# A gated mix of softmax attention and a feature-map attention on one core: 91 instead of 79 offloaded exponential packs, with other rules and values for the planner

## The chip, the cores and the metric

The kernel runs on 1 core of one Trainium2 chip. The metric is the device time of one launch in microseconds, the median of several runs. The profile is one execution, taken by the hardware profiler; its span is the time from the first to the last instruction on the core.

## The reference

Cut and shortened. Two attention branches share one input of 2048 rows and 512 columns in bfloat16, with 32 heads of 16 columns. Branch A is softmax attention: 32 heads x 2048 x 2048 scores are exponentiated. Branch B is a linear attention whose feature map is a softmax over 16 columns. A gate for each row mixes the two.

```python
def _A_ref(x, wqkv, wo):
    q, k, v = ...                                   # (1, 32, 2048, 16) each
    scores = jnp.einsum("bhqd,bhkd->bhqk", q, k) * (Dh ** -0.5)
    p = _softmax(scores, axis=-1)
    o = jnp.einsum("bhqk,bhkd->bhqd", p, v)
    return o.transpose(0, 2, 1, 3).reshape(B, S, D) @ wo

def _B_ref(x, wqkv, w_phi, wo):
    pq, pk = q @ w_phi, k @ w_phi                   # per head, 16 x 16
    phi_q = concatenate([softmax(pq), softmax(-pq)])
    phi_k = concatenate([softmax(pk), softmax(-pk)])
    kv, z = phi_k^T v, sum of phi_k over s
    return (phi_q kv / (phi_q z + 1e-6)) @ wo

g = sigmoid((x * gate_w).sum(-1))
return g * _A_ref(...) + (1 - g) * _B_ref(...)
```

## The kernel before, in words

**Tiles.** Branch A goes through 32 tiles n, each of 512 queries (one of four chunks) and four heads. A tile has 16 key blocks kt of 128 keys; a key block has four score matrices of 128 keys x 512 queries, one for each head, which are called units. The main chain (main_chain, line 831 on) takes units in groups of 2 and 3. For each group TensorE writes the scores to a ring of five PSUM banks (ps_ring, L885), ScalarE exponentiates them to a ring of 20 slots in SBUF (ET, L903), and TensorE multiplies them with the values, which have a column of ones for the row sums, into ps_ot (L942). At a tile's end VectorE transposes ps_ot (L1079) and divides by the row sums (L1081, L1082, L1090).

**Packs.** Some key blocks of a tile do not go to ScalarE: dve_pack (line 970 on) takes a whole key block, four units, through VectorE and GpSimd. DVE_COUNT says how many packs a tile has, 79 in all. The steps of a pack:

- four score matmuls into the two banks of ps_mp (L992), each evacuated by VectorE to 32-bit integers EW, scaled so that the upper half holds the exponent and the lower half the fraction (L997);
- Ef, the fraction as a float16 (L1024), in pieces of 512 or 1024 columns. The planner may put each piece on GpSimd or on VectorE; SHAPE and PIECES give the sizes;
- ED, the exponent part shifted to bfloat16's place (L1028), on GpSimd alone, in pieces of 512 or 1024 columns;
- a polynomial in Ef on VectorE in three steps that depend on each other: Em = Ef x Ef (L1033), Em = E3 x Em + E1 (L1035), Ef = Ef x Em as an integer (L1037);
- a DMA with integer addition, issued by GpSimd, that adds Ef onto ED in SBUF (L1040, 512 KB); ED, read as bfloat16, is then the exponential;
- four matmuls with the values into ps_ot (L1050).

There are 2 buffers of EW, 3 of Ef, 3 of ED and one of Em; packs follow each other in order through Em (ed_prev).

**Other work.** The projections of q, k and v (L728, L807 with their evacuations L745, L777, L812, L827), the whole of branch B (feature, query_b) and the output projection (L1269, L1290) are spread over the same time. Branch B uses VectorE (L1204, L1206, L1236 to L1240), ScalarE (L1192) and transposing DMAs on the SP queue (L1212, L1245). The SP queue also places q by DMA (L763).

**The planner.** No order is written out by hand. Each step is an operation with an engine, an estimated duration, a release time, a priority, the buffers that it takes and frees, and what it depends on. Sched.run is a list scheduler: it steps through modelled time and always gives the engine that is free first its ready operation of lowest priority number. The order in which it places operations is the order of each engine's instructions; times exist only in the model, and on the chip each instruction waits for semaphores. Fillers (L961, spare_mm) are zero matmuls that the planner puts in TensorE's idle time.

The planner models one shared resource of VectorE and GpSimd, which it calls the port: operations on SBUF data (port=True on VectorE, all of GpSimd's) exclude each other, through hold["dve"] and hold["pool"]. An operation with gate=True is parked until VectorE has work that does not need the port, or has nothing to do, for long enough; it is then also made to wait for the VectorE instruction ahead of that gap (c.war.append(last)). In the kernel before, the DMA of a pack is such an operation.

What a DMA costs in the model comes from SWD = [issue on GpSimd in us, bytes, latency in us]; bytes are spread at 250 KB/us over a common DMA time, so that later DMAs queue behind earlier ones. A pack's release and priority come from its tile's start and end in modelled time (tn), LEAD[0] and LEAD[1], and from the tables by tile OFF, PRI, POLY; LEAD[6] is the priority offset of its last matmuls. AFF, SHY, FILL and SLIP are thresholds by tile in the scheduler's choices.

The time of the chain's start and the length of a unit in the model are PACE.

## Time and profile before

| | |
|---|---|
| median of 3 runs | 875.87 us (872.78 to 876.44) |
| the profiled execution's own time | 876.78 us |
| its span | 874.9 us |
| mean granted TensorE clock | 0.988 |
| instructions | 15147 |
| DMA moved | 67.46 MB, mean 77 GB/s |

The profile names engines PE (TensorE matmuls), PEld (its weight loads), DVE (VectorE), ACT (ScalarE), POOL (GpSimd) and SP (SyncE, whose queue issues DMAs). A row of a group gives line, engine, operation, output and input with shapes, the count, and then busy time in us, mean duration of one in ns, and the idle time of the engine ahead of them with what ended most of it. Busy time is a union: instructions that overlap on one engine count once, so that busy time divided by the count is what one instruction costs in a dense run, and is below its mean duration. In the waits a row is who waited, for whom, and then us in total, times, and the longest. In a time line a row is start, length, engine, line, and in brackets the engine's idle time just before and what ended it. In the busy time by stretch a row is the stretch, its length, then the busy time of PE, PEld, DVE, ACT and POOL with instruction counts, the granted clock, the DMA engines' share and GB/s.

### The profile page before, as it was taken

What the parts mean: (1) busy time and instruction counts of PE and PEld (TensorE: products, weight loads), DVE (VectorE), ACT (ScalarE), POOL (GpSimd) and SP (SyncE); (2) the same over time, 40 slices, a digit from 0 to 9 for tenths busy, and PEclk for the clock granted to TensorE, in tenths of its full rate; (3) what the DMA queues carried; (4) which work ended last, traced back from release to release, by engine and by line L of the source; (5) the groups of instructions that cost most, each with busy time, mean ns of one, the idle gap of its engine ahead of it and who ended that gap; (6) DMA issues with size and microseconds to landing.
All of it is one profiled execution on the core that took longest, in us unless ns stands there. A gap on an engine that the chain in (4) does not pass through costs nothing.

```text
span 874.9 us, 15147 instructions
## 1 busy us (share of the span) xinstructions
PE 798.2 (91%) x6241; PEld 237.8 (27%) x6241; DVE 719.8 (82%) x1030; ACT 822.0 (94%) x765; POOL 322.3 (37%) x394
## 2 busy tenths in 40 slices
PE   8989999899999999899997899988988998989998
PEld 3333322233333322222221222222222222222222
DVE  6889889867679998995984998889788898988843
ACT  6995999999999999699996999899999999999997
POOL 2425344411114433433441454322435444363421
PEclk9998999999999999999997999999999999999999
DMA  6352541534324444544155334544423525432331
GB/s 141 78 91 61 100 72 31 98 64 76 64 52 93 82 82 82 103 82 94 40 105 67 64 65 90 82 88 70 94 58 68 103 49 88 83 76 52 76 73 49
DMA packets 94292, 67.46 MB, mean 77 GB/s; under 512 B 76560, under 2 KB 84112, under 8 KB 94224
## 3 DMA queue, kind: packets, MB, share of 16 engines
q0 software_dynamic: 11376, 41.42, 24.7%
q1 hardware_dynamic: 81504, 24.55, 14.8%
q8 instruction: 49, 0.80, 0.4%
q10 hardware_dynamic: 1344, 0.52, 0.2%
q14 instruction: 19, 0.16, 0.1%
HBM read 3.69 MB, written 2.10 MB: 7 GB/s over the span
## 4 chain that ended last, share of the span: by engine, by line
ACT 74%; DVE 9%; DMA 8%; PE 8%; issue 1%; POOL 0%; SPq 0%; POOLq 0%
ACT ET L903 70%; DMA ED<-Ef 5%; ACT phi L1192 3%; DVE EW L997 3%; PE ps_ring L885 2%; DMA phiT<-phi 2%; PE ps_ot L942 1%; DVE Ef L1024 1%; PE ps_ot L961 1%; DVE Em L1033 1%; DVE T L1082 1%; PE ps_mp L992 1%; PE ps_mp L728 1%; PE ps_ot L1050 1%; DMA WA<-in_A_wqkv_dram 1%
## 5 line engine op out<-in xcount | busy, mean ns | idle before, releaser
L903 ACT ACTIVATE ET<-ps_ring 128x1024 bf16<-128x1024 f32 (+1 forms) x693 | 793.0, 1314 | 40.9 <-PE ps_ot L942 22.6
L885 PE MATMUL ps_ring<-qT,kT 64*128 64x512 bf16 x1732 | 347.1, 386 | 45.4 <-ACT ET L903 34.2
L1028 POOL TENSOR_SCALAR ED<-EW 128x512 int16<-128x512 int16 (+1 forms) x256 | 210.5, 888 | 267.0 <-DVE Ef L1037 88.9
L997 DVE TENSOR_SCALAR EW<-ps_mp 128x512 int32<-128x512 f32 x316 | 204.7, 683 | 44.9 <-PE ps_mp L992 43.9
L961 PE MATMUL ps_ot<-zero,iden 64*128 64x512 bf16 (+2 forms) x680 | 152.7, 381 | 0.0
L885 PEld LDWEIGHTS ps_ring<-qT,kT 64*128 64x128 bf16 x1732 | 72.0, 93 | 286.6 <-ACT ET L903 263.5
L1040 POOL DMA_DIRECT2D ED<-Ef x79 | 70.9, 913 | 191.3 <-DVE Ef L1037 62.0
L942 PE MATMUL ps_ot<-ET,Vaug 128*17 128x512 bf16 x1732 | 136.5, 384 | 1.5 <-DVE T L1079 1.5
L992 PE MATMUL ps_mp<-qT,kT 64*128 64x512 bf16 (+1 forms) x316 | 112.5, 387 | 8.3 <-DVE EW L997 4.0
L1033 DVE TENSOR_TENSOR Em<-Ef 128x2048 f16<-128x2048 f16 x79 | 101.7, 1288 | 2.2 <-POOL Ef L1024 1.4
L1037 DVE TENSOR_TENSOR Ef<-Ef,Em 128x2048 int16<-128x2048 f16 x79 | 97.4, 1233 | 0.8
L1024 DVE TENSOR_SCALAR Ef<-EW 128x1024 f16<-128x1024 uint16 (+1 forms) x121 | 85.1, 713 | 3.2 <-DMA ED<-Ef 2.8
L1024 POOL TENSOR_SCALAR Ef<-EW 128x1024 f16<-128x1024 uint16 (+1 forms) x51 | 48.0, 941 | 78.2 <-DVE EW L997 47.9
L1035 DVE TENSOR_SCALAR Em<-Em 128x2048 f16<-128x2048 f16 x79 | 58.6, 742 | 0.9
L961 PEld LDWEIGHTS ps_ot<-zero,iden 64*128 64x128 bf16 (+2 forms) x680 | 48.3, 96 | 37.7 <-issue 1.1
L942 PEld LDWEIGHTS ps_ot<-ET,Vaug 128*17 128x17 bf16 x1732 | 26.7, 87 | 80.1 <-issue 68.1
L992 PEld LDWEIGHTS ps_mp<-qT,kT 64*128 64x128 bf16 (+1 forms) x316 | 28.9, 95 | 63.4 <-DVE EW L997 34.5
L1206 DVE TENSOR_TENSOR phi<-phi,frec 128x1024 bf16<-128x1024 bf16 x32 | 42.1, 1317 | 0.3
L728 PE MATMUL ps_mp<-Wp,xT 128*128 128x512 bf16 x128 | 39.3, 384 | 0.3 <-DVE EW L997 0.2
L728 PE MATMUL ps_mp<-xT,WA 128*128 128x512 bf16 (+1 forms) x128 | 38.0, 378 | 1.1 <-DMA WA<-in_A_wqkv_dram 0.6
L1192 ACT ACTIVATE phi<-ps_mp 128x512 bf16<-128x512 f32 x64 | 37.2, 679 | 1.0 <-PE ps_mp L728 1.0
L1050 PE MATMUL ps_ot<-ED,Vaug 128*17 128x512 bf16 x316 | 31.5, 389 | 6.2 <-DMA ED<-Ef 6.0
(90 smaller groups left out, 398.5 us busy)
## 6 DMA issues: line engine op xcount, KB each, us to landing
ED<-Ef POOLq DMA_DIRECT2D x79, 512.0 KB, 4.8
qT<-qst SPq DMA_DIRECT2D x120, 16.0 KB, 1.8
out_dram<-outt SPq DMA_DIRECT2D x12, 128.0 KB, 1.7
WA<-in_A_wqkv_dram SPq DMA_DIRECT2D x3, 384.0 KB, 4.4
phiT<-phi SPq DMA_TRANSPOSE x48, 3.2
WBV<-in_B_wqkv_dram SPq DMA_DIRECT2D x1, 512.0 KB, 6.5
Wp<-in_A_wo_dram SPq DMA_DIRECT2D x1, 512.0 KB, 4.1
WBV<-in_B_wo_dram SPq DMA_DIRECT2D x1, 512.0 KB, 5.9
```

What stands on the lines that cost most here:

```text
L728: m = s.op("pe", self.c_mm(n), lambda e, c=c: e.matmul(self.bk(b)[:, 0:n], lhs(c), rhs(c), start=(c == 0), stop=(c == 3)), deps if c == 0 ...
L885: return lambda e: e.matmul(self.ps_ring[:, x % RING, :], self.kT[r, g // 2, kt * P:(kt + 1) * P], self.qT[r, n % 2, i, :], start=True, st ...
L903: self.o_exp.append(s.op("act", w * 0.434 + 0.045, lambda e, b0=b0, s0=s0, w=w: e.activation(self.ET[:, s0:s0 + w, :], self.ps_ring[:, b0: ...
L942: return lambda e: e.matmul(self.ps_ot[32 * i:32 * i + VSL, :], self.Vaug[:, kt, h, :], self.ET[:, (4 * p + k) % NSLOT, :], start=(kt == 0 ...
L961: return lambda e: e.matmul(self.ps_ot[c:c + nc, :], self.iden[r:r + nr, 0:nc], self.zero[r:r + nr, :], start=False, stop=False, tile_posi ...
L992: return lambda e: e.matmul(bank(), self.kT[r, cp, kt * P:(kt + 1) * P], self.qT[r, n % 2, i, :], start=True, stop=True, tile_position=(r. ...
L997: return s.op("dve", dur, lambda e: e.tensor_scalar(self.EW[:, ew.idx, x * QCH:(x + w) * QCH], src(), float(EC), float(127 * 65536), op0=A ...
L1024: fs = [s.op("pool", U * 8.26e-4 + 0.28, lambda e, c=c: e.tensor_scalar(self.Ef[:, ef.idx, U * c:U * c + U], half(0, dt.uint16, c, U), flo ...
L1028: hs = [s.op("pool", W * 8.26e-4 + 0.165, lambda e, c=c: e.tensor_scalar(self.ED[:, ed.idx, W * c:W * c + W].bitcast(dt.int16), half(1, dt ...
L1033: u = s.op("dve", 1.13, lambda e: e.tensor_tensor(self.Em[:], Ef(), Ef(), ALU.mult), fs + [self.ed_prev], pr, port=True)
L1037: g_ = s.op("dve", 1.13, lambda e: e.tensor_tensor(Ef().bitcast(dt.int16), Ef(), self.Em[:], ALU.mult), [q], pr, port=True)
L1040: v = s.op("pool", SWD[0], lambda e: e.dma_start(out().bitcast(dt.int16), Ef().bitcast(dt.int16), accum_op=ALU.add), [g_] + hs, pr, frees= ...
```

## The change

The change has four parts. DVE_COUNT gives 13 tiles one or two packs more and two tiles one less, 91 packs in all for 79. The planner no longer counts a DMA on GpSimd as a user of the port. The DMA of a pack is no longer gated. And SWD and the tables have other values: the model's issue takes 0.65 us instead of 1.1, the latency 1.6 us instead of 2.5, and the bytes are 662500 instead of 524288; packs are released 30 us ahead of their place in the tile instead of 16.5 (LEAD[0]), with 5.0 instead of 8.7 added for their priority (LEAD[1]). No instruction computes anything else than before, and no buffer is added.

```diff
-LEAD = [16.455462617506317, 8.705434360851719, 19.141216454617272, 18.856826992452106, 21.376333972175523, 40.540151693083416, 4.775252756783429, 13.0]
-PACE = [0.8933644759852923, 0.45802931388055307]
+LEAD = [30.0, 5.0, 19.141216454617272, 18.856826992452106, 21.376333972175523, 40.540151693083416, 4.775252756783429, 13.0]
+PACE = [0.8749384591637832, 0.45792738439677627]
...
-SWD = [1.1, 524288, 2.5]
+SWD = [0.65, 662500, 1.6]
...
-DVE_COUNT = (1, 3, 2, 2, 2, 3, 2, 2, 1, 2, 3, 3, 2, 3, 2, 3, 2, 3, 3, 2, 3, 3, 2, 3, 3, 2, 3, 3, 3, 3, 3, 2)
+DVE_COUNT = (1, 3, 3, 2, 3, 4, 2, 2, 1, 3, 4, 2, 3, 2, 3, 3, 4, 3, 3, 3, 3, 3, 3, 3, 3, 3, 3, 3, 3, 3, 4, 3)
...
-        self.port = port or eng == "pool"
+        self.port = port or (eng == "pool" and not dma)
...
         v = s.op("pool", SWD[0], lambda e: e.dma_start(
             out().bitcast(dt.int16), Ef().bitcast(dt.int16), accum_op=ALU.add), [g_] + hs, pr, frees=[ef],
-            gate=gate, dma=SWD[1])
+            dma=SWD[1])
```

One of RULES and many of the values of AFF (all zero before), OFF, PRI, SHY, FILL, SLIP, POLY and SHAPE differ too. What all of this makes of the program is seen in the order of its instructions, which is known before it runs. By the order, the changed kernel has 338 exponentials of two units and 336 of three (before 347 and 346), 91 of each of L1033, L1035, L1037 and L1040 (before 79), 364 evacuations L997 (316), 104 wide and 41 narrow Ef pieces on VectorE (109 and 12), 40 wide and 35 narrow ones on GpSimd (35 and 16), 300 ED pieces (256), and 463 fillers (680). SP's queue has the same DMAs.

Three places show how the order moves. The first is GpSimd's queue in the middle of the program, around the DMA of the last pack of tile 18 (tiles count from 0), the first of the pair here; ED and Ef are the pack's buffers, whose numbers are left out. Before:

```order
L1028 TENSOR_SCALAR ED<-EW 128x512
L1040 DMA ED<-Ef 128x2048
L1024 TENSOR_SCALAR Ef<-EW 128x1024 x2
L1028 TENSOR_SCALAR ED<-EW 128x1024 x2
L1040 DMA ED<-Ef 128x2048 x2
L1028 TENSOR_SCALAR ED<-EW 128x1024 x2
L1040 DMA ED<-Ef 128x2048
```

And now, around the same pack, whose DMA is the second of the two here:

```order
L1024 TENSOR_SCALAR Ef<-EW 128x1024
L1028 TENSOR_SCALAR ED<-EW 128x512 x3
L1040 DMA ED<-Ef 128x2048
L1024 TENSOR_SCALAR Ef<-EW 128x1024
L1028 TENSOR_SCALAR ED<-EW 128x512
L1040 DMA ED<-Ef 128x2048
L1028 TENSOR_SCALAR ED<-EW 128x512 x3
```

Two DMAs that stood behind each other now have conversions of a following pack between them. Before, 10 of the 79 DMAs directly follow another one; now none does.

The second place is VectorE's queue ahead of the second transposition of ps_ot (L1079), the end of tile 1; gden, gcol, wphi and Wp belong to the gate and to branch B's weights. Before:

```order
L1033 TENSOR_TENSOR Em<-Ef 128x2048
L1035 TENSOR_SCALAR Em<-Em 128x2048
L1037 TENSOR_TENSOR Ef<-Ef,Em 128x2048
L1112 TENSOR_SCALAR gden<-gneg 128x16
L1113 RECIPROCAL gcol<-gden 128x16
L812 CAST Vaug<-ps_mp 128x4x8x16
L997 TENSOR_SCALAR EW<-ps_mp 128x512 x2
L1116 TENSOR_TENSOR wphi<-wphc,m_52 128x512
L997 TENSOR_SCALAR EW<-ps_mp 128x512 x2
L1024 TENSOR_SCALAR Ef<-EW 128x512
L1130 CAST Wp<-ps_mp 128x4x128
L997 TENSOR_SCALAR EW<-ps_mp 128x512 x4
```

Two L1130 and the transposition follow. And now:

```order
L1033 TENSOR_TENSOR Em<-Ef 128x2048
L1035 TENSOR_SCALAR Em<-Em 128x2048
L1037 TENSOR_TENSOR Ef<-Ef,Em 128x2048
L1079 STREAM_TRANSPOSE T_77<-ps_ot 128x512
L1112 TENSOR_SCALAR gden<-gneg 128x16
L1081 RECIPROCAL rinv<-T_77 128x16
L1113 RECIPROCAL gcol<-gden 128x16
L1116 TENSOR_TENSOR wphi<-wphc,m_52 128x512
```

The transposition has moved ahead of the gate, of the weights and of the next packs' evacuations. Ahead of the first transposition (not shown) stand three whole chains L1033 to L1037 now, and two before.

The third place is VectorE's queue at the end of tile 17. Before:

```order
L1033 TENSOR_TENSOR Em<-Ef 128x2048
L1290 TENSOR_SCALAR outt<-ps_mp,gcol 128x512
L1035 TENSOR_SCALAR Em<-Em 128x2048
L1037 TENSOR_TENSOR Ef<-Ef,Em 128x2048
L1024 TENSOR_SCALAR Ef<-EW 128x1024
L1079 STREAM_TRANSPOSE T_77<-ps_ot 128x512
L1081 RECIPROCAL rinv<-T_77 128x16
L997 TENSOR_SCALAR EW<-ps_mp 128x512 x4
```

And now, at the same transposition:

```order
L1033 TENSOR_TENSOR Em<-Ef 128x2048
L997 TENSOR_SCALAR EW<-ps_mp 128x512 x2
L1035 TENSOR_SCALAR Em<-Em 128x2048
L1024 TENSOR_SCALAR Ef<-EW 128x1024
L997 TENSOR_SCALAR EW<-ps_mp 128x512 x3
L1079 STREAM_TRANSPOSE T_77<-ps_ot 128x512
L1081 RECIPROCAL rinv<-T_77 128x16
L1037 TENSOR_TENSOR Ef<-Ef,Em 128x2048
```

Between the steps of a chain there now stand evacuations and conversions of later packs. L1035 directly follows its L1033 in 7 of 91 chains, before in 27 of 79; behind L1037 comes an evacuation L997 in 34 cases, a conversion L1024 in 19.

More of the change, by code (lines that the diff above doesn't have):

```diff
@@ L30 @@
 PASSES = 1
-LEAD = [16.455462617506317, 8.705434360851719, 19.141216454617272, 18.856826992452106, 21.376333972175523, 40.540151693083416, 4.775252756783429, 13.0]
-PACE = [0.8933644759852923, 0.45802931388055307]
+LEAD = [30.0, 5.0, 19.141216454617272, 18.856826992452106, 21.376333972175523, 40.540151693083416, 4.775252756783429, 13.0]
+PACE = [0.8749384591637832, 0.45792738439677627]
 BOUNDS = [3.0710501327799653, 8.000889564597248, 7.971137937737645, 18.02257936663145, 29.86797202712817]
-RULES = [0.14805191866515324, 0.5274031413498357, 0.09512931304184667]
+RULES = [0.1498235423970469, 0.5274031413498357, 0.09512931304184667]
 PIECES = ((2, 2), (2, 4), (4, 4))
@@ new lines @@
+PRI = [-2.5977761809841518, 12.575398704445774, 3.895376356683779, 2.074886791441081, -6.1760123019027215, 0.0, 0.4457880973056989, 12.368950578623885, 7.524264789393655, -1.888923368598384, -5.057883055897609, 4.784017942556362, 0.7346491630142227, 0.0, 2.0007432723814103, 0.0, -8.964017875209546, -6.817875849305981, -12.903739516547825, 10.87669422388445, 2.941617488397717, -4.250877620548464, 5.900872194940888, -12.246670183932817, -8.652806589559093, 2.1291175144482652, -5.675434887761552, -0.8975021592515438, -7.6958394115627495, -4.167683124616095, -8.873737501331755, 12.096931011196038, 0.0]
@@ L49 @@
+SHAPE = [2, 0, 2, 2, 2, 1, 1, 2, 2, 1, 1, 0, 0, 1, 0, 0, 2, 1, 0, 1, 0, 0, 0, 1, 1, 0, 1, 1, 1, 0, 1, 2, 1]
 VSL = 17
```

14 lines of the change are left out of this document (6 added, 8 removed).

## The prediction

> **What bounds the kernel now.** I read the page first, then ScalarE's waits and time line, then the busy time by stretch. From the page, the busy times and the chain that ended last:
>
> ```profile
> PE 798.2 (91%) x6241; PEld 237.8 (27%) x6241; DVE 719.8 (82%) x1030; ACT 822.0 (94%) x765; POOL 322.3 (37%) x394
> ...
> ACT 74%; DVE 9%; DMA 8%; PE 8%; issue 1%; POOL 0%; SPq 0%; POOLq 0%
> ```
>
> ScalarE is busy for 822.0 of 874.9 us and holds three quarters of the chain: it is the bound, and 52.9 us of its idle time are the rest. Who it waited for, and then, from its time line, the four long waits (in brackets) and a long stretch without any:
>
> ```profile
> ACT ET L903 <- PE ps_ot L942: 22.6, 4, 9.8
> ACT ET L903 <- PE ps_ring L885: 16.8, 15, 6.7
> ```
>
> ```profile
> 74.81 13.71 ACT L903 ACTIVATE ET<-ps_ring 128x1536 bf16<-128x1536 f32 x12 [9.84 <-PE ps_ot L942]
> ...
> 359.46 3.28 ACT L903 ACTIVATE ET<-ps_ring 128x1024 bf16<-128x1024 f32 x3 [6.64 <-PE ps_ot L942]
> ...
> 468.89 2.54 ACT L903 ACTIVATE ET<-ps_ring 128x1536 bf16<-128x1536 f32 x2 [6.70 <-PE ps_ring L885]
> ...
> 550.58 12.75 ACT L903 ACTIVATE ET<-ps_ring 128x1536 bf16<-128x1536 f32 x11 [5.04 <-PE ps_ot L942]
> ...
> 736.15 131.43 ACT L903 ACTIVATE ET<-ps_ring 128x1536 bf16<-128x1536 f32 x116 [1.15 <-PE ps_mp L992]
> ```
>
> The last row gives the exponential's price: 131.43 / 116 = 1.133 us an instruction, and these alternate between 2 and 3 tiles, so 0.453 us a tile. The four waits hold 28.2 us. Now VectorE's share, by stretch (columns: length, then PE, PEld, DVE, ACT, POOL):
>
> ```profile
> 0.00:844.00 844.00, 771.01 (x6071) 230.55 (x6071) 707.00 (x1009) 796.48 (x742) 317.91 (x390) 0.99 0.41 78
> 844.00:874.90 30.90, 27.15 (x170) 7.24 (x170) 12.78 (x21) 25.54 (x25) 4.41 (x4) 1.00 0.17 43
> ```
>
> ```profile
> 287.20:337.20 50.00, 47.24 (x381) 14.29 (x380) 48.85 (x72) 48.96 (x47) 17.49 (x20) 1.00 0.45 82
> 279.60:379.60 100.00, 91.84 (x750) 28.16 (x747) 95.13 (x136) 90.34 (x86) 37.24 (x47) 1.00 0.43 82
> 297.30:361.30 64.00, 58.20 (x471) 17.97 (x471) 59.74 (x88) 55.31 (x53) 23.66 (x29) 1.00 0.47 92
> ```
>
> On the whole VectorE has 18% to spare, but where the packs stand densely it is the fuller engine: 97.7% over 50 us, 95.1% over 100 us, 93.3% over 64 us, and there ScalarE idles. How full VectorE can be kept is what this change depends on.
>
> **The change part by part.** First, ScalarE loses work. The order has 338 + 336 exponentials of two and three tiles instead of 347 + 346, so 48 tiles less: 48 x 0.453 = 21.8 us. ScalarE alone: 874.9 - 21.8 = 853.1 us, if its waits keep their sum.
>
> Second, VectorE gains 12 packs. Its groups by form (busy, mean ns | idle before):
>
> ```profile
> L997 DVE TENSOR_SCALAR EW<-ps_mp 128x512 int32<-128x512 f32 x316 | 204.7, 683 | 44.9 <-PE ps_mp L992 43.9
> ...
> L1033 DVE TENSOR_TENSOR Em<-Ef 128x2048 f16<-128x2048 f16 x79 | 101.7, 1288 | 2.2 <-POOL Ef L1024 1.4
> L1037 DVE TENSOR_TENSOR Ef<-Ef,Em 128x2048 int16<-128x2048 f16 x79 | 97.4, 1233 | 0.8
> ...
> L1024 DVE TENSOR_SCALAR Ef<-EW 128x1024 f16<-128x1024 uint16 x109 | 80.2, 746 | 3.2 <-DMA ED<-Ef 2.8
> ...
> L1035 DVE TENSOR_SCALAR Em<-Em 128x2048 f16<-128x2048 f16 x79 | 58.6, 742 | 0.9
> ...
> L1024 DVE TENSOR_SCALAR Ef<-EW 128x512 f16<-128x512 uint16 x12 | 5.0, 415 | 0.0
> ```
>
> 48 evacuations x 204.7/316 = 31.1; 12 chains x (101.7 + 97.4 + 58.6)/79 = 39.1; the Ef conversions go from 109 wide and 12 narrow to 104 and 41, so 29 x 0.415 - 5 x 0.736 = 8.4. Together 78.6 us: VectorE has 798.4 us to do, ScalarE 822.0 - 21.8 = 800.2. The two come out level, and none of the 78.6 us lies beside idle time that is sure to be there.
>
> So the sum goes by VectorE. The last 30.9 us are a drain in which it idles; I keep them. Ahead of them it does 707.0 + 78.6 = 785.6 us. At the 100-us share that takes 785.6 / 0.9513 = 825.8; with the drain 856.7. The ends are 0.977 (835.0) and 0.933 (872.5). I take the middle row, as it is the longest stretch and holds one of the four waits. 856.7 is more than ScalarE's 853.1, so VectorE sets the end, by a little. The profiled execution took 876.78 us, 1.9 over its span, and the median shown is 875.87, so I add 1.0 to a span: **857.7 us**; ScalarE's path gives 854.1.
>
> Third, the engines beside them. From the page:
>
> ```profile
> L1028 POOL TENSOR_SCALAR ED<-EW 128x512 int16<-128x512 int16 (+1 forms) x256 | 210.5, 888 | 267.0 <-DVE Ef L1037 88.9
> ...
> L961 PE MATMUL ps_ot<-zero,iden 64*128 64x512 bf16 (+2 forms) x680 | 152.7, 381 | 0.0
> ...
> L1040 POOL DMA_DIRECT2D ED<-Ef x79 | 70.9, 913 | 191.3 <-DVE Ef L1037 62.0
> ...
> L1024 POOL TENSOR_SCALAR Ef<-EW 128x1024 f16<-128x1024 uint16 (+1 forms) x51 | 48.0, 941 | 78.2 <-DVE EW L997 47.9
> ```
>
> GpSimd: 44 x 0.822 + 24 x 0.941 + 12 x 0.897 = 69.6 more, 392 us or 46%: hidden, if the conversions stay in VectorE's gaps (the slower rival says what if not). TensorE swaps 96 matmuls for 96 and holds 152.7 us of fillers that give way: nothing.
>
> Fourth, the gate goes. Five L1037 and five L1040 start in the first 75 us (the count of L1037 is the first row), and packs keep their order, so the last of each belong together. The chain ends at 59.73 us and its DMA starts 14.8 us later, since it had to stand in a gap of VectorE:
>
> ```profile
> 0.00:75.00 75.00, 6.10 (x5) 0.95 0.49 101
> ```
>
> ```profile
> 58.50 1.23 DVE L1037 TENSOR_TENSOR Ef<-Ef,Em 128x2048 int16<-128x2048 f16 x1
> ...
> 74.53 0.89 POOL L1040 DMA_DIRECT2D ED<-Ef  x1 [1.98 <-DVE Wp L1130]
> ```
>
> What TensorE paid for late sums is small, and where two DMAs went out together (ten times before, never after) they landed late, here in 7.7 us against a median of 4.8:
>
> ```profile
> PEld ps_ot L1050 <- DMA ED<-Ef: 12.0, 14, 2.0
> ...
> PE ps_ot L1050 <- DMA ED<-Ef: 6.0, 10, 1.5
> ```
>
> ```profile
> DMA to landing us min/median/max: 4.4/4.8/9.3
> ```
>
> ```profile
> ED<-Ef POOLq DMA_DIRECT2D x2, 512.0 KB, 7.7
> ```
>
> So the lift is worth between 0 and 18 us on TensorE, and nothing of it reaches a full VectorE; I take 0. Against it stand 12 more DMAs. Two of ScalarE's waits (6.70 and 5.04) follow a transposition of phi, issued within 0.1 us of such a DMA, that took 8.72 and 6.26 us instead of 3.2:
>
> ```profile
> 457.41 0.88 POOL L1040 DMA_DIRECT2D ED<-Ef  x1 [1.38 <-DVE phi L1206]
> ...
> 541.07 1.78 POOL L1040 DMA_DIRECT2D ED<-Ef  x2 [7.43 <-DVE Ef L1037]
> ```
>
> ```profile
> 457.45 8.72 DMA phiT<-phi
> ...
> 540.98 6.26 DMA phiT<-phi
> ```
>
> ```profile
> phiT<-phi SPq DMA_TRANSPOSE x48, 3.2
> ```
>
> With 91 DMAs for 79 the same chance gives 11.7 x 12/79 = 1.8 us more: within the rounding of the share.
>
> Fifth, the new tables. In the order, the second transposition of ps_ot now follows the third chain at once, and what stood between (gate, weights, eight evacuations) comes behind it; one more chain stands ahead of the first. The 9.84-us wait lies there. It can shrink by up to 9.84 less one pack, 78.6 / 12 = 6.6 us, or move into the first tile, where the extra chain would cost those 6.6 us if ScalarE had to wait for it. And the chain's three steps rarely follow each other directly (L1035 behind L1033: 7 of 91, before 27 of 79). Both are part of the share that VectorE reaches; I give them no term.
>
> Last, whether the DMA needs the port that the planner no longer books. Here L1035 ran from 511.92 to 512.64 and the DMA's issue from 512.03, in 0.87 us, no longer than its mean of 0.913:
>
> ```profile
> 511.92 0.72 DVE L1035 TENSOR_SCALAR Em<-Em 128x2048 f16<-128x2048 f16 x1
> 512.03 0.87 POOL L1040 DMA_DIRECT2D ED<-Ef  x1
> ```
>
> By this row the missing gate costs nothing. The Trainium skill's page "SBUF — State Buffer" (section "Who interferes with whom") says otherwise: while VectorE runs an operation in a two-port mode, GpSimd cannot write a DMA's descriptors, and the DMA waits for its end. By that rule the issue would have stood until 512.64 and shown some 1.5 us; the row does not.
>
> **The rivals.** ScalarE stays the bound. If VectorE holds 0.97 and more, as over 50 us, the time is 854.1, and down to 839 if the waits of 5.04 and 6.64 go (the DMA pairs) and 3.2 of the 9.84. For: the looser order. Against: 0.977 was held for 50 us only.
>
> VectorE only reaches 0.933: 872.5 + 1.0 = 873.5, no change to speak of. For: TensorE and VectorE wait for each other in order, and two level engines hide nothing of each other's stalls. Against: that stretch holds a 6.64-us wait of ScalarE.
>
> The DMA's issue waits for VectorE after all. Behind L1037 the order has L1024 19 times and other operations on SBUF 10 times. 29 waits of up to 0.74 us are 21.5 on GpSimd, which has room; TensorE waited for sums 24 times in 79, so 29 x 24/79 x 0.74 = 6.5 us come through: 864.2. Against it stands the row of 512.03. The rule of the Trainium skill's "SBUF — State Buffer" above would give this case.
>
> Slower than before: GpSimd's conversions hold up VectorE. The price is one row:
>
> ```profile
> 357.58 2.69 POOL L1028 TENSOR_SCALAR ED<-EW 128x512 int16<-128x512 int16 x4
> ...
> 358.56 2.26 DVE L1024 TENSOR_SCALAR Ef<-EW 128x1024 f16<-128x1024 uint16 x1 [0.57 <-DMA ED<-Ef]
> ```
>
> An operation of 0.74 us took 2.26 while GpSimd converted: 1.52 lost. There are 375 conversions for 307, and a planner that books 0.65 us for an issue of 0.9 puts them late. It turns the result from 14 such holds: (785.6 + 21.5) / 0.9513 + 31.9 = 880.3; 20 give 889.7. Against it: the conversions are still gated into gaps, only the DMA is not.
>
> That the change does not do what it says can be left out: the order has the 12 packs and lacks the 48 tiles.
>
> **How the numbers follow.** Chances: forecast 0.46 (849 to 866); ScalarE 0.20 (839 to 854); 0.933 0.16 (866 to 878); DMA 0.06; slower rival 0.12 (876 to 900). A measurement here tells 0.5% from no change: below 871.5 is faster, above 880.3 slower. Faster: 0.46 + 0.20 + 0.06 + 0.07 of the 0.933 case = 0.79; same: 0.09 + 0.02 of the slower rival = 0.11; slower: the other 0.10. The range 845 to 877 leaves out 0.05 below (of ScalarE's case) and 0.12 above.
>
> **What would show it.** ScalarE's busy time near 800 and VectorE's near 798, VectorE at 95% ahead of the drain; issues of L1040 soon behind their L1037 and still 0.9 us; no landing in pairs. Wrong if VectorE is below 93% or its L1024 and L1033 means rise (holds), or if ScalarE still waits while VectorE idles.

## The result, and the profile after

| | before | after |
|---|---|---|
| median of 4 runs each, side by side | 874.63 us (872.78 to 876.44) | 839.91 us (836.37 to 842.66) |
| ratio, 95% interval | | 0.9601 (0.9557 to 0.9645) |
| the profiled execution: time, span | 876.78, 874.9 us | 836.37, 834.6 us |
| mean granted TensorE clock | 0.988 | 0.994 |

The change makes the kernel 4.0% faster. The forecast was 857.7 us with a range of 845 to 877: the direction is right, the gain is about twice the one forecast, and the measured time lies below the range.

The page of the kernel after, its busy times and the chain that ended last:

```profile
PE 751.7 (90%) x5940; PEld 226.5 (27%) x6024; DVE 776.2 (93%) x1138; ACT 801.9 (96%) x746; POOL 385.8 (46%) x474
...
ACT 38%; DVE 35%; PE 15%; DMA 9%; issue 2%; POOL 1%; SPq 0%; ACTq 0%; POOLq 0%
```

ScalarE does 801.9 us for 822.0, 20.1 less, and idles 834.6 - 801.9 = 32.7 us for 52.9, 20.2 less. Together that is the 40.3 us between the spans: half of the gain is work taken away, and half is waiting that went. The chain is now shared between ScalarE and VectorE, where ScalarE held 74% before. ScalarE's two groups of waits after (who, for whom, us in total, times, longest):

```profile
ACT ET L903 <- PE ps_ring L885: 16.9, 25, 2.6
ACT ET L903 <- PE ps_ot L942: 2.2, 1, 2.2
```

From ScalarE's time line after, the two longest waits (in brackets) and its last long run of exponentials:

```profile
252.59 2.37 ACT L903 ACTIVATE ET<-ps_ring 128x1024 bf16<-128x1024 f32 x2 [2.44 <-PE ps_ring L885]
...
592.31 2.36 ACT L903 ACTIVATE ET<-ps_ring 128x1536 bf16<-128x1536 f32 x2 [2.61 <-PE ps_ring L885]
...
692.29 134.82 ACT L903 ACTIVATE ET<-ps_ring 128x1536 bf16<-128x1536 f32 x119 [0.15 <-PE ps_ring L885]
```

The four waits of 5 to 10 us are gone and, ahead of the drain, nothing longer than 2.61 us has come in their place. Of the two groups it is the waits for L942 that went, 22.6 us before and 2.2 now; the waits for the score matmuls L885 keep their sum, 16.8 and 16.9, in shorter pieces. The price of an exponential has not moved: 134.82 / 119 = 1.133 us. Busy time by stretch after, split at the drain:

```profile
0.00:805.00 805.00, 726.50 (x5777) 219.41 (x5857) 759.38 (x1110) 777.93 (x724) 375.38 (x462) 0.99 0.45 89
805.00:834.60 29.60, 25.22 (x164) 7.11 (x167) 16.87 (x29) 23.96 (x23) 10.43 (x13) 1.00 0.31 74
```

VectorE is busy for 759.38 / 805 = 94.3% of the time ahead of a drain of 29.6 us. VectorE's groups by form after (busy, mean ns of one, idle before):

```profile
L997 DVE TENSOR_SCALAR EW<-ps_mp 128x512 int32<-128x512 f32 x364 | 234.8, 679 | 19.9 <-PE ps_mp L992 17.5 <-PE ps_ot L1050 0.9 <-PE ps_ot L942 0.2
L1033 DVE TENSOR_TENSOR Em<-Ef 128x2048 f16<-128x2048 f16 x91 | 118.7, 1305 | 1.1 <-POOL Ef L1024 0.7
...
L1024 DVE TENSOR_SCALAR Ef<-EW 128x1024 f16<-128x1024 uint16 x104 | 75.6, 737 | 0.0
L1035 DVE TENSOR_SCALAR Em<-Em 128x2048 f16<-128x2048 f16 x91 | 64.7, 711 | 0.2
...
L1082 DVE TENSOR_TENSOR T<-T,rinv 128x256 bf16<-128x256 f32 x31 | 16.2, 524 | 0.0
```

The two rows that were to show conversions holding VectorE up have hardly moved: L1033 takes 1305 ns for 1288, the wide L1024 737 for 746. VectorE has 776.2 us to do and not 798.4. The DMAs of the packs after, as a group, and TensorE's waits for them:

```profile
L1040 POOL DMA_DIRECT2D ED<-Ef x91 | 82.5, 906 | 140.3 <-DVE Ef L1037 119.7
```

```profile
PEld ps_ot L1050 <- DMA ED<-Ef: 18.9, 38, 1.7
...
PE ps_ot L1050 <- DMA ED<-Ef: 4.8, 12, 1.2
```

GpSimd now mostly waits for L1037 itself, for 119.7 us in all. Pairing each L1037's end with the start of its own DMA, the delay was 5.7 us in the median before and is 0.3 us now. TensorE waits for sums 18.9 + 4.8 = 23.7 us, against 12.0 + 6.0 = 18.0 before: the sums come earlier, but the new order asks for them earlier too.

Whether the issue needs VectorE's port can be seen more finely than before. From GpSimd's time line after, then from VectorE's:

```profile
619.71 1.35 POOL L1040 DMA_DIRECT2D ED<-Ef  x1 [1.49 <-DVE Ef L1037]
...
701.25 0.89 POOL L1040 DMA_DIRECT2D ED<-Ef  x1 [2.57 <-DVE Ef L1037]
```

```profile
619.95 1.04 DVE L1024 TENSOR_SCALAR Ef<-EW 128x1024 f16<-128x1024 uint16 x1
...
701.48 1.21 DVE L1033 TENSOR_TENSOR Em<-Ef 128x2048 f16<-128x2048 f16 x1
```

An issue usually takes 0.886 us. Beside L1033 it took that, 0.89. Beside a conversion that ran until 620.99 it stood until 621.06. Nine issues have a wide L1024 that began within their first 0.3 us and reaches into the last tenth of a microsecond of that time; they end 0.08 to 0.14 us after that L1024 and last 0.93 to 1.35 us. Two more, with three narrow L1024 beside them, take 1.07. Three others have a wide L1024 that began 0.69 us or more into the issue; those issues took at most 0.89 us, and two of these L1024 took 1.40, with a conversion on GpSimd beside them. Of 35 issues whose last tenth lies wholly beside a tensor_tensor, none took over 0.90. So the issue does wait for VectorE's conversions, but only its last part, and here only for one that was already running: in eleven of 91 issues, for 1.9 us in all, on an engine that is idle half the time.

### The profile page after: what moved, and what is told of

It reads as the page before. It is cut to its first block, busy times and chain, and to the rows that moved or that the text cites. A ratio compares the mean times of both kernels' runs of the same rounds, so it can differ in the third digit from the quotient of the medians.

```text
span 834.6 us, 14837 instructions
## 1 busy us (share of the span) xinstructions
PE 751.7 (90%) x5940; PEld 226.5 (27%) x6024; DVE 776.2 (93%) x1138; ACT 801.9 (96%) x746; POOL 385.8 (46%) x474
## 3 DMA queue, kind: packets, MB, share of 16 engines
q0 software_dynamic: 13104, 47.72, 29.6%
## 4 chain that ended last, share of the span: by engine, by line
ACT 38%; DVE 35%; PE 15%; DMA 9%; issue 2%; POOL 1%; SPq 0%; ACTq 0%; POOLq 0%
ACT ET L903 35%; DVE EW L997 10%; DMA ED<-Ef 6%; DVE Em L1033 6%; DVE Ef L1037 6%; PE ps_ring L885 5%; DVE Ef L1024 4%; DVE Em L1035 3%; ACT phi L1192 2%; PE ps_ot L942 2%; PE ps_mp L728 2%; DMA phiT<-phi 2%; PE ps_mp L992 1%; PE ps_mp L1269 1%; DVE phi L1206 1%
## 5 line engine op out<-in xcount | busy, mean ns | idle before, releaser
L903 ACT ACTIVATE ET<-ps_ring 128x1024 bf16<-128x1024 f32 (+1 forms) x674 | 772.0, 1298 | 20.5 <-PE ps_ring L885 16.9
L885 PE MATMUL ps_ring<-qT,kT 64*128 64x512 bf16 x1684 | 339.0, 386 | 42.1 <-ACT ET L903 30.9
L1028 POOL TENSOR_SCALAR ED<-EW 128x512 int16<-128x512 int16 (+1 forms) x300 | 240.7, 833 | 231.4 <-DVE Ef L1037 61.5
L997 DVE TENSOR_SCALAR EW<-ps_mp 128x512 int32<-128x512 f32 x364 | 234.8, 679 | 19.9 <-PE ps_mp L992 17.5
L1040 POOL DMA_DIRECT2D ED<-Ef x91 | 82.5, 906 | 140.3 <-DVE Ef L1037 119.7
L885 PEld LDWEIGHTS ps_ring<-qT,kT 64*128 64x128 bf16 x1684 | 70.3, 93 | 258.9 <-ACT ET L903 233.0
L942 PE MATMUL ps_ot<-ET,Vaug 128*17 128x512 bf16 x1684 | 132.8, 384 | 1.0 <-DVE T L1079 0.6
L1033 DVE TENSOR_TENSOR Em<-Ef 128x2048 f16<-128x2048 f16 x91 | 118.7, 1305 | 1.1 <-POOL Ef L1024 0.7
L1037 DVE TENSOR_TENSOR Ef<-Ef,Em 128x2048 int16<-128x2048 f16 x91 | 115.6, 1271 | 0.3
L961 PE MATMUL ps_ot<-zero,iden 64*128 64x512 bf16 (+2 forms) x453 | 105.7, 378 | 1.4 <-issue 0.5
L1024 POOL TENSOR_SCALAR Ef<-EW 128x1024 f16<-128x1024 uint16 (+1 forms) x75 | 67.6, 902 | 62.2 <-DVE EW L997 17.4
L1024 DVE TENSOR_SCALAR Ef<-EW 128x1024 f16<-128x1024 uint16 (+1 forms) x145 | 94.4, 665 | 0.2
L1035 DVE TENSOR_SCALAR Em<-Em 128x2048 f16<-128x2048 f16 x91 | 64.7, 711 | 0.2
L942 PEld LDWEIGHTS ps_ot<-ET,Vaug 128*17 128x17 bf16 x1684 | 25.5, 87 | 77.9 <-issue 69.0
L1206 DVE TENSOR_TENSOR phi<-phi,frec 128x1024 bf16<-128x1024 bf16 x32 | 41.4, 1300 | 0.1
L961 PEld LDWEIGHTS ps_ot<-zero,iden 64*128 64x128 bf16 (+2 forms) x463 | 32.7, 95 | 22.4
```

Of the source, the lines that this page charges most:

```text
L885: return lambda e: e.matmul(self.ps_ring[:, x % RING, :], self.kT[r, g // 2, kt * P:(kt + 1) * P], self.qT[r, n % 2, i, :], start=True, st ...
L903: self.o_exp.append(s.op("act", w * 0.434 + 0.045, lambda e, b0=b0, s0=s0, w=w: e.activation(self.ET[:, s0:s0 + w, :], self.ps_ring[:, b0: ...
L942: return lambda e: e.matmul(self.ps_ot[32 * i:32 * i + VSL, :], self.Vaug[:, kt, h, :], self.ET[:, (4 * p + k) % NSLOT, :], start=(kt == 0 ...
L961: return lambda e: e.matmul(self.ps_ot[c:c + nc, :], self.iden[r:r + nr, 0:nc], self.zero[r:r + nr, :], start=False, stop=False, tile_posi ...
L997: return s.op("dve", dur, lambda e: e.tensor_scalar(self.EW[:, ew.idx, x * QCH:(x + w) * QCH], src(), float(EC), float(127 * 65536), op0=A ...
L1024: fs = [s.op("pool", U * 8.26e-4 + 0.28, lambda e, c=c: e.tensor_scalar(self.Ef[:, ef.idx, U * c:U * c + U], half(0, dt.uint16, c, U), flo ...
```

## The experiments

Ratios are to the kernel before, run on the same chip (its medians there were 877 to 879 us). The kernels fall in two kinds. In some the order of the instructions is exactly that of before or of after and only waits or the size of an operation differ, or the fillers are left out. In others the planner makes a new order, whose quality the tables alone can shift by a per cent or more; those say less of a single cause. The granted clock differs too: it is 0.988 before and 0.994 after, but 0.849 to 0.985 in the kernels below that are slower than before, so part of what they lose may be the clock; how much was not separated.

### The gate, in the order of before

The kernel before; each DMA keeps its place in GpSimd's queue and loses only its wait for the gap (at both places):

```diff
-                if last is not None:
+                if last is not None and not c.dma:
                     c.war.append(last)
```

> The kernel before with every instruction in its old order; only the 78 gated DMAs no longer wait for the VectorE instruction ahead of their gap, so that they start when their own data are ready. Theory EARLY (what was gained beside the 21.8 us of ScalarE's work comes from sums that land sooner): ScalarE's two waits behind late sums (6.64 and 5.04 us) go and TensorE's 18.0 us of waits for sums shrink, 863 to 867 us. Theory PLAN (the gain beside the work comes from the order that the planner makes once a DMA is cheap for it): 871 to 877 us, as before, since TensorE and GpSimd still have their old order.

Measured: 0.9781 (0.9738 to 0.9825), 858.22 us. Page of this kernel, ScalarE's waits and TensorE's waits for sums, then one VectorE group before and here:

```profile
PE 780.5 (91%) x6162; PEld 237.4 (28%) x6241; DVE 706.0 (82%) x1030; ACT 820.8 (96%) x765; POOL 319.7 (37%) x394
```

```profile
ACT ET L903 <- PE ps_ot L942: 17.0, 4, 7.0
ACT ET L903 <- PE ps_ring L885: 6.5, 9, 1.6
...
PEld ps_ot L1050 <- DMA ED<-Ef: 1.0, 2, 0.5
```

```profile
L1082 DVE TENSOR_TENSOR T<-T,rinv 128x256 bf16<-128x256 f32 x31 | 18.5, 597 | 0.4
```

```profile
L1082 DVE TENSOR_TENSOR T<-T,rinv 128x256 bf16<-128x256 f32 x31 | 13.7, 442 | 0.4
```

The lift alone, with the same instructions in the same order, gives 2.2%: more than either theory had for it, and it was costed at nothing. ScalarE's idle time falls from 52.9 to 857.0 - 820.8 = 36.2 us. The median delay from a chain to its DMA falls only from 5.7 to 4.3 us, yet two things change with it. TensorE's waits for sums fall from 18.0 to 1.0 us, as theory EARLY had it, although ScalarE's waits of 6.64 and 5.04 us do not go: they are still 6.16 and 2.79. And VectorE does the same 1030 instructions in 13.8 us less; L1082 falls from 597 to 442 ns.

The second can be followed in the traces. Added up over each kernel, GpSimd's conversions (L1024, L1028) run beside VectorE's operations on SBUF (L1024, L1033, L1035, L1037, L1082, L1206) for 71.3 us before and for 52.4 us here. That fits a DMA which, while it waits for a gap, holds the conversions behind it in GpSimd's queue back too, out of the gaps that the planner meant for them; what conversions outside of gaps cost is measured further down. How much of ScalarE's gain came through the sums and how much through VectorE, this run does not separate. The granted clock is 0.996 for 0.988; at the price of the run without fillers at the end of the experiments (0.046 of clock for 1.5%) that makes an estimated 0.3%, so it is not the bulk.

### Packs, rules and tables apart

The kernel before with only the new DVE_COUNT, 91 packs:

```diff
-DVE_COUNT = (1, 3, 2, 2, 2, 3, 2, 2, 1, 2, 3, 3, 2, 3, 2, 3, 2, 3, 3, 2, 3, 3, 2, 3, 3, 2, 3, 3, 3, 3, 3, 2)
+DVE_COUNT = (1, 3, 3, 2, 3, 4, 2, 2, 1, 3, 4, 2, 3, 2, 3, 3, 4, 3, 3, 3, 3, 3, 3, 3, 3, 3, 3, 3, 3, 3, 4, 3)
```

> The kernel before with DVE_COUNT of the changed one alone (91 packs), old rules, old SWD, old tables. Theory COUNT (the packs alone bring it, ScalarE's idle time falls from 52.9 to about 33 us because the load of the tiles is level): 838 to 845 us. Theory PLAN: ScalarE's busy time falls by 21.8 us to 800, but its idle time stays at 53 us or grows, 853 to 868 us.

Measured: 1.0797 (1.0752 to 1.0842), 948.38 us. Its page and its two longest groups of ScalarE's waits:

```profile
PE 843.0 (89%) x6389; PEld 258.8 (27%) x6478; DVE 798.3 (84%) x1132; ACT 802.4 (85%) x746; POOL 372.8 (39%) x454
```

```profile
ACT ET L903 <- PE ps_ot L942: 85.1, 19, 13.6
ACT phi L1192 <- PE ps_mp L728: 27.4, 6, 12.7
```

Worse than both theories. The packs alone cost 8%. That VectorE's 798.3 us meets the 798.4 of the forecast's sum is chance: this kernel has 119 wide and 20 narrow L1024 on VectorE, where the sum had 104 and 41.

The kernel after with the old DVE_COUNT, 79 packs:

```diff
-DVE_COUNT = (1, 3, 3, 2, 3, 4, 2, 2, 1, 3, 4, 2, 3, 2, 3, 3, 4, 3, 3, 3, 3, 3, 3, 3, 3, 3, 3, 3, 3, 3, 4, 3)
+DVE_COUNT = (1, 3, 2, 2, 2, 3, 2, 2, 1, 2, 3, 3, 2, 3, 2, 3, 2, 3, 3, 2, 3, 3, 2, 3, 3, 2, 3, 3, 3, 3, 3, 2)
```

> The changed kernel with the old DVE_COUNT (79 packs). ScalarE's work is then 822 us again. Theory PLAN: its idle time stays near the 33 us of the changed kernel, 822 + 33 + 2 = 857 us. Theory COUNT: its idle time is back at 50 us and more, 872 to 878 us.

Measured: 0.9898 (0.9847 to 0.9949), 869.16 us, between the theories' numbers. ScalarE's work is back to 823.4 us:

```profile
PE 788.3 (90%) x6147; PEld 235.8 (27%) x6224; DVE 703.3 (81%) x1025; ACT 823.4 (94%) x765; POOL 337.4 (39%) x415
```

The kernel before with the new rules (port, gate, SWD) and otherwise old values:

```diff
-SWD = [1.1, 524288, 2.5]
+SWD = [0.65, 662500, 1.6]
...
-        self.port = port or eng == "pool"
+        self.port = port or (eng == "pool" and not dma)
...
-            gate=gate, dma=SWD[1])
+            dma=SWD[1])
```

> The kernel before with the planner's new rules for the DMA alone (no port, no gate, SWD 0.65, 662500, 1.6); 79 packs and all old tables. If the rules alone free ScalarE's 20 us of waits: 853 to 858 us. If the tables do: 870 to 877 us. Between the two, both do.

Measured: 0.9916 (0.9882 to 0.9950), 871.05 us. At 79 packs the new tables therefore change nothing that can be told (0.9898 with them), and a new order gives less than lifting the waits in the old one.

The kernel after with the old rules, the same three edits the other way round:

```diff
-SWD = [0.65, 662500, 1.6]
+SWD = [1.1, 524288, 2.5]
...
-        self.port = port or (eng == "pool" and not dma)
+        self.port = port or eng == "pool"
...
-            dma=SWD[1])
+            gate=gate, dma=SWD[1])
```

> The changed kernel with the planner's old rules for the DMA (port, gate, SWD 1.1, 524288, 2.5); 91 packs and all new tables. Theory RULES (91 packs only pay because the DMA is cheap and free for the planner; the old rules with 91 packs and old tables took 948): over 900 us. Theory TABLES (the new tables make room for the packs): 845 to 870 us.

Measured: 1.0504 (1.0461 to 1.0547), 922.3 us:

```profile
PE 841.4 (91%) x6524; PEld 256.5 (28%) x6524; DVE 776.6 (84%) x1130; ACT 802.8 (87%) x746; POOL 392.9 (43%) x482
```

VectorE and ScalarE have as much to do as in the kernel after (776.2 and 801.9; on VectorE eight conversions fewer) and the launch takes 82 us longer. So the amount of work on either does not say when the kernel ends.

The kernel before with the new rules and the new DVE_COUNT, and the old tables: the edits of the first and third of this part together (DVE_COUNT and the port's line are cut here).

```diff
-SWD = [1.1, 524288, 2.5]
+SWD = [0.65, 662500, 1.6]
...
-            gate=gate, dma=SWD[1])
+            dma=SWD[1])
```

> The kernel before with the new rules for the DMA and with 91 packs; all old tables. Theory RULES: 845 to 860 us, most of the gain of the changed kernel. Theory TABLES: 870 us and more, since the old tables time the packs for 79.

Measured: 1.0027 (0.9997 to 1.0057), 880.86 us:

```profile
PE 800.4 (90%) x6188; PEld 238.5 (27%) x6188; DVE 780.4 (88%) x1121; ACT 803.2 (91%) x746; POOL 385.4 (43%) x465
```

The seven kernels as a table:

| packs | rules | tables | ratio |
|---|---|---|---|
| 79 | old | old | 1 |
| 79 | new | old | 0.9916 |
| 79 | new | new | 0.9898 |
| 91 | old | old | 1.0797 |
| 91 | new | old | 1.0027 |
| 91 | old | new | 1.0504 |
| 91 | new | new | 0.9601 |

At 79 packs the rules are worth 1%; at 91 packs 7% with the old tables (1.0027 / 1.0797) and 9% with the new (0.9601 / 1.0504). The packs only pay with both. 79 packs under old rules with new tables were not run.

### Which of the rules

The kernel after, with only the gate put back, then with only the old SWD:

```diff
-            dma=SWD[1])
+            gate=gate, dma=SWD[1])
```

> The changed kernel with the gate of the DMA back, and nothing else (no port for the DMA in the model, new SWD). If the gate is the rule that matters: 880 us and more, near the 922 of all old rules. If the model's price and port matter more: 838 to 860 us.

Measured: 1.0376 (1.0321 to 1.0431), 910.16 us.

```profile
PE 828.7 (91%) x6289; PEld 247.6 (27%) x6289; DVE 778.9 (86%) x1134; ACT 804.8 (88%) x746; POOL 386.9 (42%) x478
```

```diff
-SWD = [0.65, 662500, 1.6]
+SWD = [1.1, 524288, 2.5]
```

> The changed kernel with the old model price of the DMA (SWD 1.1, 524288, 2.5) and without gate and port. If the lifted gate is what matters: 838 to 855 us. If the price is: over 870 us.

Measured: 1.0293 (1.0227 to 1.0360), 900.4 us.

```profile
PE 809.4 (90%) x6156; PEld 238.3 (27%) x6156; DVE 788.6 (88%) x1136; ACT 804.5 (90%) x746; POOL 382.0 (42%) x476
```

Each alone loses the whole gain and more. With the gate back the median delay from chain to DMA is 6.3 us again. With the old SWD it stays 0.3 us, as after: there the loss lies in the order itself, perhaps because the planner books more for a DMA than it takes; that reason is argued, not shown. Both are new orders under tables that belong to another setting, so part of each loss may be that. The third rule, the port, was not put back alone.

### Waits added and taken in the order of after

The kernel after, its order unchanged; GpSimd's conversions lose their waits for VectorE's gaps:

```diff
-                if last is not None:
+                if last is not None and c.dma:
                     c.war.append(last)
```

> The changed kernel with every instruction in its order; GpSimd's conversions no longer wait for the VectorE instruction ahead of their gap, as its DMAs already do not. If conversions that start outside their gap hold up VectorE (the slower rival's mechanism): its busy time rises by 10 us or more and the time to 850 to 870 us. If GpSimd's earlier start is worth more, as for the DMAs of the old order (878 to 858): 825 to 837 us. If neither: 837 to 843 us.

Measured: 1.0573 (1.0485 to 1.0662), 931.33 us. Two VectorE groups and ScalarE's first wait of this kernel:

```profile
L1033 DVE TENSOR_TENSOR Em<-Ef 128x2048 f16<-128x2048 f16 x91 | 158.2, 1738 | 1.5 <-POOL Ef L1024 1.1
...
L1024 DVE TENSOR_SCALAR Ef<-EW 128x1024 f16<-128x1024 uint16 x104 | 96.6, 939 | 0.0
```

```profile
ACT ET L903 <- PE ps_ring L885: 89.8, 81, 3.5
```

This is the slower rival's mechanism, switched on: L1033 goes from 1305 to 1738 ns and the wide L1024 from 737 to 939, VectorE does the same instructions in 858.3 us instead of 776.2, and the kernel is slower than before. GpSimd's conversions now run beside VectorE's operations on SBUF for 218.1 us instead of 84.6, counted as above. In the kernel after, the gap waits that the conversions kept hold it off. The Trainium skill's page "SBUF — State Buffer", section "Who interferes with whom", describes it: VectorE and GpSimd share a pair of ports, and where a VectorE operation in a two-port mode, or one with two inputs in SBUF, meets a GpSimd operation that needs the pair, whichever comes first makes the other wait for its whole length. The rows agree that VectorE's operations take longer when conversions run beside them; as means they do not show the length of a single wait, and no trace here shows an operation's mode.

The kernel after with its order unchanged; each DMA also waits for the sixth VectorE instruction behind its chain, then for the second (LATE is 6, then 2; a nearer one is taken where the order would close a circle; the diff is cut to the loop that adds the waits):

```diff
+        k = max(at[d] for d in o.deps if d.eng == "dve")
+        for n in range(LATE, 0, -1):
...
+            d = dve[k + n]
...
+                o.war.append(d)
```

> The changed kernel with every instruction in its order; each pack's DMA is made to wait for the sixth VectorE instruction behind its own chain (or the furthest one that makes no circle), as a gate would. Theory EARLY (the early DMA is worth 16 to 20 us by itself, as in the old order): 856 us and more, with VectorE busy 10 us longer. Theory PLAN (only the order matters): 838 to 846 us.

> The changed kernel in its order; each pack's DMA waits for the second VectorE instruction behind its chain instead of none (1.2 us or so; the sixth one gave 1108 us). If what a late DMA costs goes by its delay past the planned landing: 850 to 900 us. If a short delay is absorbed: 838 to 846 us.

Measured: 1.2615 (1.2553 to 1.2676), 1107.89 us, and 1.0280 (1.0221 to 1.0339), 906.76 us. TensorE's waits for sums, first with six, then with two:

```profile
PEld ps_ot L1050 <- DMA ED<-Ef: 180.7, 66, 6.5
...
PE ps_ot L1050 <- DMA ED<-Ef: 154.5, 59, 6.2
```

```profile
PEld ps_ot L1050 <- DMA ED<-Ef: 69.2, 54, 5.3
...
PE ps_ot L1050 <- DMA ED<-Ef: 48.8, 38, 4.8
```

In one and the same order, a median delay of 0.3, 2.0 and 5.4 us of the DMA gives 840, 907 and 1108 us, with 23.7, 118.0 and 335.2 us of TensorE waiting for sums. The order of after has no slack for a late sum. The order of before had some: there 5.7 us of delay showed as 18.0 us of such waits. The side effect on VectorE is here again, the other way round: its same 1138 instructions take 776.2, 790.4 and 817.1 us, with GpSimd's conversions beside its operations on SBUF for 84.6, 92.5 and 123.6 us.

### Which engine binds after

The kernel after, with L1035 on half its columns; half of that polynomial step is left out. Then with exponentials on 480 of 512 columns from unit 40 on, which leaves out a sixteenth of them. Then both, and both without fillers:

```diff
-            self.Em[:], self.Em[:], E3, E1, op0=ALU.mult, op1=ALU.add), [u], pr, port=True)
+            self.Em[:, 0:1024], self.Em[:, 0:1024], E3, E1, op0=ALU.mult, op1=ALU.add), [u], pr, port=True)
```

> The changed kernel in its order, with the middle step of the chain (L1035) on half of its columns: this leaves out half of the multiply-and-add of every pack. VectorE has about 91 x 0.3 = 27 us less to do. Theory VECTORE (VectorE sets the end, as the prediction had it): 812 to 822 us. Theory SCALARE (ScalarE sets it): 836 to 842 us. If the two share it: 825 to 835 us.

```diff
-            self.o_exp.append(s.op("act", w * 0.434 + 0.045, lambda e, b0=b0, s0=s0, w=w: e.activation(
-                self.ET[:, s0:s0 + w, :], self.ps_ring[:, b0:b0 + w, :], ACT.Exp, scale=float(DH) ** -0.5),
+            self.o_exp.append(s.op("act", w * 0.434 + 0.045, lambda e, b0=b0, s0=s0, w=w, c=480 if ua >= 40 else 512: e.activation(
+                self.ET[:, s0:s0 + w, 0:c], self.ps_ring[:, b0:b0 + w, 0:c], ACT.Exp, scale=float(DH) ** -0.5),
```

> The changed kernel in its order, with every exponential from unit 40 on over 480 of its 512 columns: this leaves out one column in sixteen. ScalarE has about 1644 x 0.434 / 16 = 45 us less to do. Theory SCALARE: 795 to 805 us. Theory VECTORE: 836 to 842 us. If the two share it: 810 to 830 us.

> The changed kernel in its order with both reliefs at once (L1035 on half of its columns, exponentials on 480 of 512 columns from unit 40 on; that work is left out). Each relief alone moved the time by less than 1%. Theory LEVEL (ScalarE and VectorE each bound the kernel at about the same time): 812 to 822 us (27 us less on VectorE, 32 less on ScalarE by its profile). Theory TENSORE (the in-order queue of TensorE, whose fillers are placed for the planned pace, is a third bound): 830 to 840 us.

```diff
-                    out.append(z)
+                    z.cols = z.cols
```

> As the one before, and without the zero matmuls that fill TensorE's idle time (463 fewer matmuls; the rest in its order). Theory TENSORE: under 820 us where the one before is over 830. Theory LEVEL: as the one before, within 5 us.

Measured: 0.9547 (0.9501 to 0.9593), 0.9609 (0.9524 to 0.9695), 0.9453 (0.9400 to 0.9507) and 0.9460 (0.9410 to 0.9511), against 0.9601 of the kernel after. Page and chain of the first three, in this order:

```profile
PE 765.7 (91%) x6024; PEld 224.9 (27%) x6024; DVE 751.6 (90%) x1138; ACT 800.6 (95%) x746; POOL 378.8 (45%) x474
...
ACT 65%; DVE 12%; PE 11%; DMA 9%; issue 1%; POOL 0%; SPq 0%; ACTq 0%
```

```profile
PE 768.6 (91%) x6024; PEld 228.0 (27%) x6024; DVE 774.7 (92%) x1138; ACT 769.9 (91%) x746; POOL 386.2 (46%) x474
...
DVE 54%; PE 25%; DMA 14%; ACT 3%; issue 2%; POOL 1%; SPq 0%; ACTq 0%; POOLq 0%
```

```profile
PE 753.6 (91%) x5940; PEld 227.6 (27%) x6024; DVE 750.8 (90%) x1138; ACT 766.3 (92%) x746; POOL 378.5 (46%) x474
...
DVE 38%; PE 31%; ACT 13%; DMA 12%; issue 3%; POOL 2%; SPq 0%; ACTq 0%; POOLq 0%
```

TensorE's waits for sums with ScalarE relieved, and the granted clock with both relieved, first with the fillers and then without:

```profile
PEld ps_ot L1050 <- DMA ED<-Ef: 37.8, 42, 2.7
...
PE ps_ot L1050 <- DMA ED<-Ef: 22.4, 27, 2.3
```

```profile
core 0: 829.6 us, clock 0.977
```

```profile
core 0: 824.4 us, clock 0.967
```

VectorE relieved of 24.6 us: the chain goes to ScalarE and the time falls by 0.5%, within the intervals. ScalarE relieved of 32.0 us (45 were expected): the chain goes to VectorE and the time does not move. Both relieved: 1.5% less, about 13 us, and 830.17 us, above the 812 to 822 expected of two level engines and at the lower edge of the 830 to 840 expected if TensorE were next. The two engines are level, and neither alone sets the end; yet of the 25.4 us taken from VectorE and the 35.6 from ScalarE only 13 come through. What takes the rest is open; TensorE has 31% of that chain and DMAs 12%. Two things on record may bear on it. TensorE's waits for sums grow from 23.7 us to 60.2 with ScalarE relieved and to 46.1 with both. And the granted clock, 0.994 in the kernel after, is 0.981 with ScalarE relieved and 0.977 with both. Leaving the fillers out as well does not change the time, but the clock falls again, to 0.967, and the next run shows that a lower clock costs time: so this run does not say whether the fillers hold TensorE's queue up.

The fillers alone, taken out of the kernel after (the edit just shown):

> The changed kernel in its order without the fillers (463 fewer matmuls that add zero). If the fillers hold TensorE's queue up: 825 to 836 us, a version better than both. If the clock that TensorE is granted falls without them: 845 us and more, with a granted clock below 0.95. If neither: 836 to 843 us.

Measured: 0.9745 (0.9710 to 0.9780), 856.74 us, 1.5% above the kernel after. Its clock and its score matmuls, and then the same two of the kernel after:

```profile
core 0: 854.6 us, clock 0.948
```

```profile
L885 PE MATMUL ps_ring<-qT,kT 64*128 64x512 bf16 x1684 | 354.4, 402 | 77.8 <-ACT ET L903 67.0 <-issue 0.8 <-DVE phi L1206 0.7
```

```profile
core 0: 834.6 us, clock 0.994
```

```profile
L885 PE MATMUL ps_ring<-qT,kT 64*128 64x512 bf16 x1684 | 339.0, 386 | 42.1 <-ACT ET L903 30.9
```

Without the 463 fillers TensorE's granted clock is 0.948 instead of 0.994 and a score matmul takes 402 instead of 386 ns. TensorE is not one of the two engines that the chain is shared between, but its speed reaches the end.

## Why the prediction was right in direction and wrong in size

**ScalarE's work.** 21.8 us less were forecast, 20.1 measured: right. "ScalarE alone: 853.1, if its waits keep their sum" failed by its condition: the sum of its idle time fell from 52.9 to 32.7.

**The gate: a step that failed.** "So the lift is worth between 0 and 18 us on TensorE, and nothing of it reaches a full VectorE; I take 0." The bounds were about right and the choice of 0 was wrong. In the old order the lift alone takes 17.9 us off the span (874.9 to 857.0), 2.2% of the time. The waits that the working had found do go, 18.0 us to 1.0, and VectorE's own durations, which the working did not look at, fall by 13.8 us, because fewer conversions run beside them; the two were not separated. "Nothing of it reaches a full VectorE" fails in the new order too: there the gate put back costs 8% (1.0376 for 0.9601, in an order made anew), with VectorE's work the same within 2.7 us (778.9 for 776.2). So there the gate acts through waiting, and the DMA delays added to one order (0.3, 2.0, 5.4 us) show how: the new order needs its sums early.

**The tables: another term put at nothing.** "Both are part of the share that VectorE reaches; I give them no term." At 91 packs under the new rules they are worth 1.0027 against 0.9601, 4%. At 79 packs they are worth nothing measurable. The places named there were right in this: the 9.84-us wait ahead of the second transposition is gone, and no wait of 6.6 us came into the first tile.

**VectorE sets the end: the term that was mis-sized.** The sum gave a span of 856.7 us, and 834.6 were measured. The share was sized well, 0.943 for 0.9513, and the drain too, 29.6 for 30.9. The amount was not: 776.2 us for 798.4 in all, and 759.4 for 785.6 ahead of the drain, which at the forecast's share is 27.5 us of time. Of the 22 us, 4.6 are an error of the sum: counted from each start to the next, the added pieces come to 74.0 us at the old prices, not 78.6, since groups that overlap each other were counted whole. The other 17.6 are the same instructions at a lower price. Only some 5 of these are shorter durations (L1035 711 ns for 742, L1082 524 for 597, L997 679 for 683); the rest is that each instruction starts sooner behind the one ahead and overlaps more with it, 76.7 us of overlap among 1138 instructions for 57.6 among 1030. The rules are not needed for that: the kernel with the old rules and the new tables has 776.6 us, with eight conversions fewer. And "So the sum goes by VectorE" does not hold: with the same 776 us of VectorE work the kernel with old rules takes 922 us, and with 24.6 us less of it the new one gains at most what the intervals allow. The share, which came out as forecast, did so only with the rules and the tables together: over the whole span VectorE is busy for 93% in the kernel after, 88% with the old tables and 84% with the old rules. It is an outcome of the order, not a property that a new order inherits from a row of the old one, and that the row of 100 us met it is in part luck.

**The port.** "By this row the missing gate costs nothing": the conclusion held, the row was no evidence. That L1035 ended at 512.64 and the issue at 512.90, and it is the last tenth of a microsecond of an issue that waits. The rule of the Trainium skill's "SBUF — State Buffer" (section "Who interferes with whom"), that GpSimd writes no descriptors while VectorE is in a two-port operation, agrees with the eleven issues that ended behind a conversion, 1.9 us in all, where the rival had 21.5 us on GpSimd and 6.5 at the end.

**The rivals.** ScalarE as the bound gave 839 to 854 and holds the measured time, but by luck: its condition, VectorE at 0.97, was not met. The 0.933 case and the slower rival did not come; the latter's price is real (5.7% above before without the conversions' gap waits), its trigger was absent, as the nearly unchanged L1024 and L1033 showed. Its 14 holds of 1.52 us make 21.3 us, not 21.5. The "12 more DMAs, 1.8 us" can't be told apart in these runs; no two DMAs go out together any more.

**What stays open.** Through which engine the lifted gate reaches ScalarE, which coupling holds the last part once both engines are relieved, and how much of the losses of re-planned kernels comes of tables made for other settings and of their lower clock.

## What to carry to other kernels

A wait that is found in the rows should not be put at nothing because another engine is expected to be full: here the 18.0 us of waits for sums were costed at 0, and taking the gate out in the unchanged order gave 17.9 us, though perhaps not all of it through these waits. That test, the same order with only the waits changed, prices such a step; it also shows side effects on a neighbouring engine that no wait row names. More work for a spare engine pays only if the order around it is made anew; here the same 12 packs gave +8.0, +5.0, +0.3 or -4.0% with nothing else changed but rules and tables. When two engines come out level, a sum over either is no forecast; test by relieving each, and then both, and read the granted clock of each run.

## What the hardware showed that was not expected

- In the kernel after, a software-issued accumulating DMA (0.886 us on GpSimd) waits for a tensor_scalar of VectorE that writes float16 only at the end of its issue, and then ends 0.08 to 0.14 us behind it (11 of 91 issues); with a tensor_tensor beside its end it is not lengthened (35 of 35 at most 0.90 us).
- The same VectorE instructions cost 706.0 or 719.8 us, and 776.2 or 858.3 us, depending on how long GpSimd's conversions run beside them (52.4 or 71.3 us, and 84.6 or 218.1); L1082 took 442 or 597 ns in the first pair.
- 463 zero matmuls on a TensorE that is 90% busy hold the granted clock at 0.994 instead of 0.948, worth 1.5% of the launch.
